# An eleventh 1 MB slot in the memory of a P buffer and a q buffer, with a free order of V groups and shorter norm, FFN and output steps

## The chip, the cores and the metric

The kernel runs on one core of a Trainium2 chip. The metric is the device time of one execution in microseconds (us), as a median of several executions. Profiled executions report a *span*, from the first to the last instruction, which is about 2 us less than the device time.

Five engines matter in the text: PE (matrix products), DVE (vector), ACT (activation), POOL, and SP, which here does nothing but issue loads. The loads themselves run on 16 DMA engines.

## The reference

Two layers of grouped-query attention over a KV cache, each followed by a SwiGLU FFN. There are four batch rows with one query token each. Both layers read **the same** K and V caches and the same weights.

```python
x = A_x                                              # (4, 1, 512) bf16
x = x + A(layernorm(x), A_k_cache, A_v_cache, A_wq, A_wo)
x = x + B(layernorm(x), B_w_gate, B_w_up, B_w_down)
x = x + A(layernorm(x), A_k_cache, A_v_cache, A_wq, A_wo)
x = x + B(layernorm(x), B_w_gate, B_w_up, B_w_down)
# A: q = x @ wq, 32 heads of 128; softmax(q k^T / sqrt(128)) v; @ wo
#    k_cache, v_cache: (4 batch, 8 kv heads, 8192, 128), each 64 MB; 4 q heads per kv head
# B: (silu(x @ w_gate) * (x @ w_up)) @ w_down, inner size 1792
```

K and V together are 128 MB. The SBUF holds a small part of that, so almost all of it is read twice: 256 blocks of 1 MB, less those blocks of V that a plan keeps in SBUF from layer 1 to layer 2.

## The kernel before

K and V come in 1 MB blocks into a pool of 10 slots. A block is half of the 8192 positions of one (batch, kv head). DVE transposes K blocks in place, PE multiplies them with a padded q (`qpad`) into four PSUM banks. When 16 K blocks of a batch are done, a softmax makes P in one of three `pp` buffers. Then V blocks are multiplied with P. A slot is free when PE has used it.

```python
KEPT = [5, 5, 4, 3]        # V blocks per batch that stay in their slots for layer 2: 17
NSLOT = 10
pool = sb("pool", [P, NSLOT, 2 * UE], BF16)          # 8 KB per partition and slot
pp = sb("pp", [P, 3, NCH * 512], BF16)               # three P buffers, 4 KB each
qpad = sb("qpad", [P, 2, NES, G, 32], BF16)          # two q buffers, 2 KB each
qs1 = sb("qs1", [P, NES, G, REP, B], BF16)           # layer-1 q of all batches, 1 KB
```

The whole program is straight-line. Before it is emitted, a planner in the kernel's own Python simulates it: each step has an engine, an assumed duration and dependencies, loads are taken in the fixed `ORDER`, and each load waits for the next free slot. The planned start times give each engine its instruction order.

```python
class Plan:
    PAGE = 6.2; PAGE_N = 256         # the plan's assumption: no more than 256 PE instructions in 6.2 us
    LOAD_LEAD = 0.8; LOAD_TAIL = 1.4
    ...
            s.start = t              # issue: when a slot is free
            dma_at = max(dma_at, t + self.LOAD_LEAD) + s.us
            s.end = dma_at + self.LOAD_TAIL
...
def load_pair(u):
    ...
        T.dma("sp", pool[:, s, :], src, sem_slot[s], writes=[f"slot{s}_0", f"slot{s}_1"])
    return PL.load(2.5, fn, u)
```

The V order follows from the `KEPT` numbers by rule: whole groups (kv heads), both halves of a group one after the other. Between the layers of one batch lies a *chain*: output projection, layer norm, FFN, layer norm, new q. The norm takes the mean with one matrix product, centers, squares, and takes the variance with a second one:

```python
def layer_norm(dep, tag):
    m = col_sum(XT, mean, "x", "mean", [dep], tag + "m")     # PE + DVE reduce
    def center(): ...                                        # xnT, dT, sqT: three DVE steps
    c = PL.add("dve", 0.5, center, [m], CHAIN)
    v = col_sum(sqT, var, "sqT", "var", [c], tag + "v")      # PE + DVE reduce
    ...
```

The softmax's maximum over partitions goes DVE reduce, PE transpose, DVE reduce of one row, PE broadcast, DVE copy. The result is transposed back by four PE instructions and written out as 4 rows.

Of the kernel before, what the change touches and what calls it, by code (L numbers as in the profile page):

```python
# [114 lines left out]
class Plan:  # L115

    HOP = 0.06
    PAGE = 6.2
    PAGE_N = 256
    LOAD_LEAD = 0.8  # L120
    LOAD_TAIL = 1.4
# [19 lines left out]
    def run(self):  # L141
# [15 lines left out]
        sp_at = 0.0  # L157
# [96 lines left out]
    def emit(self):  # L254
        for s in sorted(self.steps + self.loads, key=lambda s: (s.start, s.prio[0])):
# [3 lines left out]
ORDER = ("VKdVKqKKKVKKKKKKKgKKKKVoVVKKKVKKKKVKKKVuKVVVVKVKuKKKVVVVgoodoVKVKVKKKKKKKKKKKKKKKVKKVVVVKVVVKKV"  # L259
         "KVKVKVKVKVKKKKVVKVVKKVKVKKVVKKVVVKKKKVVKKKKVVVVKKVKVKKKVKKVKVKKVKVVVKVKKVKVKKKVVKKKKKKVKKKKVKVK"  # L260
         "VKKVVVVVVVVVVVVVVVVVVVVKVVKVKKKKKKKKKKKKKKVVVVVVVVVVVVVVVVVV")
KEPT = [5, 5, 4, 3]
NSLOT = 10
VCUT = [1, 1, 0, 1]
NTAIL = [0, 7, 5, 2]


def bass_interleave_layers__gqa_block_cached__swiglu_ffn__decode_kernel(
# [33 lines left out]
    with ExitStack() as es:  # L302
# [7 lines left out]
        pp = sb("pp", [P, 3, NCH * 512], BF16)  # L310
        qpad = sb("qpad", [P, 2, NES, G, 32], BF16)
        qs1 = sb("qs1", [P, NES, G, REP, B], BF16)
# [3 lines left out]
        identf = sb("identf", [P, P], FP32)  # L316
        selL = sb("selL", [P, 32], FP32)
        selw = sb("selw", [P, 32], FP32)
        invL = sb("invL", [P, 3, 32], FP32)
        xrow = pp[0:B, 0, 0:D]  # L320
        onesm = sb("onesm", [P, P], FP32)
        x0T = sb("x0T", [P, NQ, B], FP32)
        XT = sb("XT", [P, NQ, B], FP32)
        mean = sb("mean", [P, B], FP32)
# [5 lines left out]
        dT = sb("dT", [P, NQ, B], FP32)  # L330
        sqT = sb("sqT", [P, NQ, B], FP32)
        xnT = sb("xnT", [P, NQ * B], BF16)
        negm = sb("negm", [P, 3, 4], FP32)
        lsum = sb("lsum", [P, 3, 4], FP32)
        gm = sb("gm", [P, 1], FP32)
        gl = sb("gl", [P, 1], FP32)
        alpha = sb("alpha", [P, 3, 4], FP32)
        wl = sb("wl", [P, 4], FP32)
        rowm = sb("rowm", [1, P], FP32)
        one1 = sb("one1", [1, 1], FP32)  # L340
# [5 lines left out]
        xoT = sb("xoT", [P, NQ * B], BF16)  # L346
# [6 lines left out]
        def bank_bf(k):  # L353
# [16 lines left out]
        op("pool", lambda e: e.memset(identf[:], 0.0), writes=["identf"])  # L370
        op("pool", lambda e: e.affine_select(out=identf[:], in_=identf[:], pattern=[[-1, P]],
                                             compare_op=ALU.not_equal, fill=1.0, base=0,
                                             channel_multiplier=1),
           reads=["identf"], writes=["identf"])
        op("pool", lambda e: e.memset(qpad[:], 0.0), writes=["qpad0_0", "qpad0_1", "qpad1_0", "qpad1_1"])
        op("pool", lambda e: e.memset(oT[:], 0.0), writes=[f"oT{l}_{g}" for l in range(2) for g in range(G)])
        op("dve", lambda e: e.memset(one1[:], 1.0), writes=["one1"])
        op("dve", lambda e: e.memset(eps_sb[:], EPS), writes=["eps"])
        op("dve", lambda e: e.memset(onesm[:], 1.0 / D), writes=["onesm"])
        op("dve", lambda e: e.tensor_copy(ident[:], identf[:]), reads=["identf"], writes=["ident"])  # L380
        T.dma("sp", xrow, A_x.rearrange("b s d -> (b s) d"), sem_x, writes=["xrow"])
        nc.scalar.preload_act_table_set("natural_log_exp_and_others")

        def setup_late():
            for j in range(4):
                op("dve", lambda e: e.tensor_scalar(selL[32 * j:32 * (j + 1), :],
                                                    identf[32 * j:32 * (j + 1), 32 * j:32 * (j + 1)],
                                                    float(D), None, op0=ALU.mult),
                   reads=["identf"], writes=["selL"])
# [9 lines left out]
        def over_nq(t):  # L399
            a = t[:]  # L400
            return bass.AP(tensor=a.tensor, offset=a.offset, ap=[[a.ap[0][0], P], [0, NQ], [1, B]])
# [8 lines left out]
        def col_sum(src, dst, key_in, key_out, deps, tag):  # L410
            def mm():
                bk = pbk(tag)
                op("pe", lambda e: e.matmul(ps[:, bk * BW:bk * BW + NQ * B], lhsT=onesm[:],  # L413
                                            rhs=src[:].rearrange("p n b -> p (n b)"), start=True, stop=True),
                   reads=["onesm", key_in], writes=[f"pb{bk}"])

            def rd():
                bk = pbk(tag)
                op("dve", lambda e: e.tensor_reduce(dst[:], ps[:, bk * BW:bk * BW + NQ * B].rearrange("p (n b) -> p b n", b=B),  # L419
                                                    AX.X, ALU.add), reads=[f"pb{bk}"], writes=[key_out])  # L420
            a = PL.add("pe", 0.6, mm, deps, CHAIN, take=tag, n=8)
            return PL.add("dve", 0.17, rd, [a], CHAIN, free=tag)

        def layer_norm(dep, tag):
            m = col_sum(XT, mean, "x", "mean", [dep], tag + "m")

            def center():
                op("dve", lambda e: e.tensor_tensor(xnT[:].rearrange("p (n b) -> p n b", b=B), XT[:], over_nq(mean),
                                                    ALU.subtract), reads=["x", "mean"], writes=["xnT"])
                op("dve", lambda e: e.tensor_tensor(dT[:], XT[:], over_nq(mean), ALU.subtract),  # L430
                   reads=["x", "mean"], writes=["dT"])
                op("dve", lambda e: e.tensor_tensor(sqT[:], dT[:], dT[:], ALU.mult), reads=["dT"], writes=["sqT"])
            c = PL.add("dve", 0.5, center, [m], CHAIN)
            v = col_sum(sqT, var, "sqT", "var", [c], tag + "v")

            def root():
                op("act", lambda e: e.activation(lnv[:], var[:], ACTF.Ln, bias=eps_sb[:], scale=1.0),  # L437
                   reads=["var", "eps"], writes=["lnv"])
                op("act", lambda e: e.activation(rstd[:], lnv[:], ACTF.Exp, scale=-0.5), reads=["lnv"], writes=["rstd"])
            return c, PL.add("act", 0.55, root, [v], CHAIN)  # L440
# [39 lines left out]
        def make_qpad1(b, dep, prior):  # L480
            k = kpos[(0, b)] % 2

            def fn():
                op("dve", lambda e: e.tensor_copy(q_diag(k, 0, G), qs1[:, :, :, :, b]),
                   reads=["qs1"], writes=[f"qpad{k}_0", f"qpad{k}_1"])
            st = PL.add("dve", 0.23, fn, [dep, prior], CHAIN)
            q_ready[(0, b)] = [st, st]

        def q_first(cen, root):
# [11 lines left out]
            s1 = PL.add("dve", 0.3, scl, [mm, qs], CHAIN, free="q0")  # L501
            sp = q_spread(qT1[:], Hq * B, "qT1", [s1], "q0s")

            def cp():
                bk = pbk("q0s")
                op("dve", lambda e: e.tensor_copy(qs1[:].rearrange("p s g j b -> p (s g j b)"), bank(bk)),
                   reads=[f"pb{bk}"], writes=["qs1"])
            return PL.add("dve", 0.7, cp, [sp], CHAIN, free="q0s")

        def q_half(b, hf, mm_tag, deps, prior):  # L510
            nh = Hq // 2
            k = kpos[(1, b)] % 2
# [24 lines left out]
        def load_pair(u):  # L537
# [8 lines left out]
            return PL.load(2.5, fn, u)  # L546
# [3 lines left out]
        p_free = {0: None, 1: None, 2: None}  # L550
# [3 lines left out]
        def k_pair(u, ld, prio, prev):  # L554
            _, l, b, g, cp = u
            qbuf = kpos[(l, b)] % 2
# [29 lines left out]
        def softmax(l, b, lastq, prio):  # L586
# [17 lines left out]
            def g1():  # L604
                op("dve", lambda e: e.tensor_reduce(gm[:], negm[:, q, :], AX.X, ALU.min),
                   reads=[f"negm{q}_{a}" for a in range(4)], writes=["gm"])
            s = PL.add("dve", 0.16, g1, [mx], CHAIN)

            def g2():
                row = ps[0:1, pbk(n + "a") * BW:pbk(n + "a") * BW + P]  # L610
                op("pe", lambda e: e.matmul(row, lhsT=gm[:], rhs=identf[:], is_transpose=True, start=True, stop=True),
                   reads=["gm", "identf"], writes=[f"pb{pbk(n + 'a')}"])
            s = PL.add("pe", 0.37, g2, [s], CHAIN, take=n + "a", n=2)

            def g3():
                row = ps[0:1, pbk(n + "a") * BW:pbk(n + "a") * BW + P]
                rep = bass.AP(tensor=row.tensor, offset=row.offset, ap=[[row.ap[0][0], 1], [0, 4], [1, 32], [32, 4]])
                op("dve", lambda e: e.tensor_reduce(rowm[:].rearrange("p (i h) -> p i h", i=4), rep, AX.X, ALU.min),
                   reads=[f"pb{pbk(n + 'a')}"], writes=["rowm"])
            s = PL.add("dve", 0.7, g3, [s], CHAIN, free=n + "a")  # L620

            def g4():
                bk = pbk(n + "b")
                op("pe", lambda e: e.matmul(ps[:, bk * BW:bk * BW + 1], lhsT=rowm[:], rhs=one1[:], start=True, stop=True),
                   reads=["rowm", "one1"], writes=[f"pb{bk}"])
            s = PL.add("pe", 0.58, g4, [s], CHAIN, take=n + "b", n=8)

            def g5():
                bk = pbk(n + "b")
                op("dve", lambda e: e.tensor_copy(gm[:], ps[:, bk * BW:bk * BW + 1]), reads=[f"pb{bk}"], writes=["gm"])  # L630
            s = PL.add("dve", 0.16, g5, [s], CHAIN, free=n + "b")
# [51 lines left out]
        opj_free = [None]  # L683

# [13 lines left out]
        def v_group(l, b, g, lds, prios):  # L698
# [3 lines left out]
            for i, cp in enumerate(VCP):  # L702
# [17 lines left out]
                if not (l == 0 and (g, cp) in kept_of[b]):  # L720
# [9 lines left out]
            if l == 0 or b == B - 1:  # L730
                wdep = [w_load[f"wo{g * REP // (Hq // 4)}"]] if l == 0 else []
                return prev, oproj(l, g, [n, opj_free[0]] + wdep, prios[1])
            return prev, n

        def ffn_mm(w_sb, wname, deps, tag):
            def fn():
                bk = pbk(tag)
                for fo in range(FO):
                    for kt in range(KT):
                        op("pe", lambda e: e.matmul(ps[:, bk * BW + fo * B:bk * BW + (fo + 1) * B],  # L740
# [4 lines left out]
                           sig=(kt == KT - 1 and fo == FO - 1))  # L745
# [268 lines left out]
```

## Time and profile before

| | before |
|---|---|
| time, median | 664.6 us |
| span | 662.4 us |
| loads of K and V | 128 + 111 |
| last landing of a load | 650.2 us |
| from there to the end ("tail") | 12.2 us |

The first view is the profile's page. The digits and GB/s cover the span in 40 equal slices; the queue lines give packets, MB and the share of 16 engines' span.

```profile
span 662.4 us, 22618 instructions
PE 459.8 (69%) x10672; PEld 276.0 (42%) x10672; DVE 375.7 (57%) x568; ACT 48.6 (7%) x114; POOL 2.7 (0%) x8
DMA  8999999999999999999999999999999999999991
GB/s 341 419 420 408 408 419 405 420 419 390 391 405 419 421 419 418 405 402 414 409 421 419 419 402 414 419 419 381 403 422 420 419 419 418 379 423 419 419 419 51
q1 hardware_dynamic: 42032, 264.53, 97.6%
q8 instruction: 83, 1.36, 0.8%
```

The DMA engines are busy everywhere but in the last slice. Most slices run at 418 to 423 GB/s; 15 between the first and the last fall below, the lowest to 379. No other engine is above 69%, so the loads bound the kernel.

The windows view of two places where the rate falls. The columns are busy time of PE, PE's weight loads, DVE, ACT and POOL in the window, then the granted PE clock, the DMA share and GB/s:

```profile
454.00:456.00 2.00, 0.60 (x24) 0.34 (x32) 2.00 (x4) 0.00 (x0) 0.00 (x0) 0.50 0.99 348
...
458.00:460.00 2.00, 1.48 (x50) 1.31 (x46) 2.00 (x4) 1.62 (x5) 0.00 (x0) 0.50 0.82 221
568.00:570.00 2.00, 1.17 (x46) 1.14 (x50) 1.07 (x3) 0.00 (x0) 0.00 (x0) 0.50 0.88 369
570.00:572.00 2.00, 2.00 (x50) 0.60 (x50) 0.85 (x1) 0.00 (x0) 0.00 (x0) 0.50 0.80 266
```

Here new q, softmax and K work meet, and the DMA share falls below 1. That reads like a queue that ran empty because slots came free late.

Pieces of the timeline (start, duration, engine, line, operation; in brackets the idle time before it and what ended it). First the softmax's maximum in the last batch, then parts of the tail:

```profile
611.56 0.16 DVE L605 TENSOR_REDUCE gm<-negm 128x1 f32<-128x4 f32 x1
612.85 0.37 PE L611 MATMUL ps<-identf,gm 128*1 128x128 f32 x1
613.26 0.68 DVE L618 TENSOR_REDUCE rowm<-ps 1x128 f32<-1x512 f32 x1
614.61 0.16 DVE L630 COPY gm<-ps 128x1 f32<-128x1 f32 x1 [0.68 <-PE ps L624]
...
650.27 1.01 PE L712 MATMUL ps<-pp,pool 128*128 128x4 bf16 x32 [1.45 <-DMA pool<-in_A_v_cache_dram]
652.17 0.17 DVE L795 TENSOR_TENSOR XT<-XT,ps 128x16 f32<-128x16 f32 x1 [0.68 <-PE ps L690]
654.23 1.63 PE L740 MATMUL ps<-xnT,wg_sb 128*128 128x4 bf16 x56
657.91 1.65 PE L782 MATMUL ps<-hT,wd_sb 128*128 128x4 bf16 x56 [0.56 <-DVE hT L775]
659.83 0.59 PE L968 MATMUL ps<-ident,xoT 128*4 128x128 bf16 x4 [0.26 <-DVE xoT L795]
660.45 0.41 DVE L975 COPY pp<-ps 4x512 bf16<-4x512 bf16 x1 [0.68 <-PE ps L968]
```

The maximum takes 3.2 us from L605 to the end of L630. The last V product waits for its load. After that load nothing is fetched any more, and 12.2 us of the last FFN follow in plain sequence.

### The profile page before, as it was taken

The page shows a single profiled execution, that of the slowest core. Times are in us where ns is not written, and L with a number is a line of the kernel's source. Part 1 is how long each engine was busy: PE and PEld are TensorE (multiplying, and loading weights), DVE is VectorE, ACT ScalarE, POOL GpSimd, SP SyncE. Part 2 cuts the span into 40 slices and gives each one's busy share as a digit, 9 for nine tenths or more (in the row PEclk, how much of TensorE's full clock was granted, in tenths as well). Part 3 has the DMA queues.
Part 4 walks back from the last instruction along what each step waited for, and adds up shares of the span by engine and source line. Part 5 has one row for each costly group of instructions (what it writes and reads, how often), then busy time and mean ns, then how long its engine had stood idle before and what let it go on. Part 6 is the DMA issues. An engine that isn't in the chain of part 4 may idle for free.

```text
span 662.4 us, 22618 instructions
## 1 busy us (share of the span) xinstructions
PE 459.8 (69%) x10672; PEld 276.0 (42%) x10672; DVE 375.7 (57%) x568; ACT 48.6 (7%) x114; POOL 2.7 (0%) x8
## 2 busy tenths in 40 slices
PE   0276487477777777996676688887876857866756
PEld 0221253326522363553332354554322756523645
DVE  4377685354389815567656385467866203697202
ACT  1000300003000110001100030001101100001100
POOL 1000000000000000000000000000000000000000
PEclk9996666555566655565656555555755555576555
DMA  8999999999999999999999999999999999999991
GB/s 341 419 420 408 408 419 405 420 419 390 391 405 419 421 419 418 405 402 414 409 421 419 419 402 414 419 419 381 403 422 420 419 419 418 379 423 419 419 419 51
DMA packets 42125, 265.97 MB, mean 401 GB/s; under 512 B 4008, under 2 KB 9904, under 8 KB 10928
## 3 DMA queue, kind: packets, MB, share of 16 engines
q1 hardware_dynamic: 42032, 264.53, 97.6%
q8 instruction: 83, 1.36, 0.8%
q14 instruction: 10, 0.08, 0.0%
HBM read 264.51 MB, written 0.00 MB: 399 GB/s over the span
## 4 chain that ended last, share of the span: by engine, by line
DMA 63%; PE 22%; DVE 11%; issue 2%; ACT 1%; SPq 1%
DMA pool<-in_A_k_cache_dram 36%; DMA pool<-in_A_v_cache_dram 25%; PE ps L574 8%; DVE pool L562 8%; PE ps L712 7%; DMA wg_sb<-in_B_w_gate_dram 2%; PE ps L650 2%; PE ps L740 1%; PE ps L451 1%; DVE negm L592 1%; SPq L92 1%; ACT pp L656 1%; PE ps L690 1%; DVE pp L641 1%; PE ps L782 1%
## 5 line engine op out<-in xcount | busy, mean ns | idle before, releaser
L562 DVE STREAM_TRANSPOSE pool<-pool 128x1024 uint32<-128x1024 uint32 x256 | 304.6, 1224 | 132.8 <-DMA pool<-in_A_k_cache_dram 128.0
L574 PE MATMUL ps<-pool,qpad 32*32 32x512 bf16 x4096 | 241.1, 563 | 65.7 <-DVE pool L562 60.6
L712 PE MATMUL ps<-pp,pool 128*128 128x4 bf16 x4096 | 126.6, 166 | 64.0 <-DMA pool<-in_A_v_cache_dram 46.8
L712 PEld LDWEIGHTS ps<-pp,pool 128*128 128x128 bf16 x4096 | 118.4, 104 | 98.6 <-DMA pool<-in_A_v_cache_dram 63.1
L574 PEld LDWEIGHTS ps<-pool,qpad 32*32 32x32 bf16 x4096 | 67.9, 112 | 187.3 <-DVE pool L562 112.5
L726 DVE TENSOR_TENSOR oT<-ps,invL 128x4 bf16<-128x4 f32 x64 | 10.1, 158 | 94.7 <-PE ps L712 94.7
L596 ACT ACTIVATE pp<-ps,negm 128x512 bf16<-128x512 f32 x32 | 21.5, 685 | 359.6 <-DVE negm L592 359.6
L451 PE MATMUL ps<-xnT,wq_sb 128*128 128x4 bf16 x640 | 18.3, 166 | 23.5 <-DMA wq_sb<-in_A_wq_dram 20.1
L690 PE MATMUL ps<-oT,wo_sb 128*128 128x4 bf16 x640 | 23.4, 167 | 10.7 <-DVE oT L726 6.2
L451 PEld LDWEIGHTS ps<-xnT,wq_sb 128*128 128x128 bf16 x640 | 18.1, 104 | 26.8 <-DMA wq_sb<-in_A_wq_dram 20.2
L690 PEld LDWEIGHTS ps<-oT,wo_sb 128*128 128x128 bf16 x640 | 20.4, 105 | 19.2 <-DVE oT L726 9.7
L592 DVE TENSOR_REDUCE negm<-ps 128x1 f32<-128x512 f32 x32 | 19.8, 677 | 9.9 <-PE ps L574 9.9
L650 PE MATMUL ps<-ident,pp 128*128 128x128 bf16 x128 | 16.5, 310 | 6.1 <-ACT pp L656 3.7
L656 ACT ACTIVATE pp<-ps 128x1024 bf16<-128x1024 bf16 x16 | 16.4, 1023 | 29.6 <-PE ps L650 29.6
L437 ACT ACTIVATE lnv<-var,eps_sb 128x4 f32<-128x4 f32 x10 | 3.0, 297 | 186.6 <-DVE var L419 186.6
L650 PEld LDWEIGHTS ps<-ident,pp 128*128 128x128 bf16 x128 | 12.3, 141 | 9.5 <-ACT pp L656 4.4
L782 PE MATMUL ps<-hT,wd_sb 128*128 128x4 bf16 x280 | 8.4, 166 | 5.2 <-issue 2.4
L782 PEld LDWEIGHTS ps<-hT,wd_sb 128*128 128x128 bf16 x280 | 7.9, 104 | 6.8 <-issue 3.9
L641 DVE TENSOR_SCALAR pp<-pp,alpha 128x512 bf16<-128x512 bf16 x32 | 9.0, 342 | 1.8 <-ACT alpha L634 1.8
L740 PEld LDWEIGHTS ps<-xnT,wg_sb 128*128 128x128 bf16 x280 | 8.2, 105 | 2.2 <-issue 2.2
L740 PE MATMUL ps<-xnT,wg_sb 128*128 128x4 bf16 x280 | 8.2, 166 | 1.3 <-DMA wg_sb<-in_B_w_gate_dram 1.3
L413 PE MATMUL ps<-XT,onesm 128*128 128x16 f32 x20 | 6.0, 382 | 3.4 <-DVE XT L795 2.9
(65 smaller groups left out, 117.8 us busy)
## 6 DMA issues: line engine op xcount, KB each, us to landing
pool<-in_A_k_cache_dram SPq DMA_DIRECT2D x128, 1024.0 KB, 10.0
pool<-in_A_v_cache_dram SPq DMA_DIRECT2D x111, 1024.0 KB, 12.9
wo_sb<-in_A_wo_dram SPq DMA_DIRECT2D x4, 1024.0 KB, 17.5
wq_sb<-in_A_wq_dram SPq DMA_DIRECT2D x1, 4096.0 KB, 20.7
wg_sb<-in_B_w_gate_dram SPq DMA_DIRECT2D x2, 896.0 KB, 18.2
wu_sb<-in_B_w_up_dram SPq DMA_DIRECT2D x2, 896.0 KB, 14.9
wd_sb<-in_B_w_down_dram SPq DMA_DIRECT2D x2, 896.0 KB, 18.8
pp<-in_A_x_dram SPq DMA_DIRECT2D x1, 4.0 KB
```

Source lines behind the costliest of these rows:

```text
L451: op("pe", lambda e: e.matmul(ps[:, bk * BW + h * B:bk * BW + (h + 1) * B], lhsT=wq_sb[:, kt, h * Dh:(h + 1) * Dh], rhs=xnT[:, kt * B:(kt ...
L562: op("dve", lambda e: e.transpose(v, v), reads=[key], writes=[key])
L574: op("pe", lambda e: e.matmul(ps[32 * c:32 * (c + 1), a * BW:(a + 1) * BW], lhsT=qpad[rows, qbuf, es_, g, :], rhs=ap[h][rows, :, es_ // 2, ...
L592: op("dve", lambda e: e.tensor_reduce(negm[:, q, a:a + 1], bank(a), AX.X, ALU.max, negate=True), reads=[f"pb{a}"], writes=[f"negm{q}_{a}"])
L596: op("act", lambda e: e.activation(pblk(q)[:, :, a, :], bank(a).rearrange("p (t j) -> p t j", j=32), ACTF.Exp, bias=negm[:, q, a:a + 1], s ...
L641: op("dve", lambda e: e.tensor_scalar(seg, seg, alpha[:, q, a:a + 1], None, op0=ALU.mult), reads=[f"pp{q}_{a}", f"alpha{q}"], writes=[f"pp ...
L650: op("pe", lambda e: e.matmul(stg[:, t * P:(t + 1) * P], lhsT=pp[:, q, blk * P:(blk + 1) * P], rhs=ident[:], is_transpose=True, start=True ...
L656: op("act", lambda e: e.activation(pp[:, q, f * 1024:(f + 1) * 1024], bank_bf(bk)[:, :], ACTF.Copy), reads=[f"pb{bk}"], writes=pk(q))
L690: op("pe", lambda e: e.matmul(ps[:, OPJ * BW + nq * B:OPJ * BW + (nq + 1) * B], lhsT=wo_sb[:, h, nq * P:(nq + 1) * P], rhs=oT[:, l, h, :], ...
L712: op("pe", lambda e: e.matmul(ps[:, bk * BW:bk * BW + REP], lhsT=ap[:, t * Dh:(t + 1) * Dh], rhs=pp[:, q, col:col + REP], start=(i == 0 an ...
L740: op("pe", lambda e: e.matmul(ps[:, bk * BW + fo * B:bk * BW + (fo + 1) * B], lhsT=w_sb[:, kt, fo * P:(fo + 1) * P], rhs=xnT[:, kt * B:(kt ...
L782: op("pe", lambda e: e.matmul(ps[:, bk * BW + nq * B:bk * BW + (nq + 1) * B], lhsT=wd_sb[:, fo, nq * P:(nq + 1) * P], rhs=hT[:, fo * B:(fo ...
```

## The change

The intent: read 4 MB less, and shorten what lies between.

- Memory: the third P buffer (4 KB), the second q buffer (2 KB), `qs1` and some small tiles make room for an eleventh slot (8 KB per partition).
- 21 V blocks are kept instead of 17, so V is 107 loads instead of 111. `ORDER` is now a list of named blocks in any order. `a` is a load for layer 1, `b` for layer 2, and `c` the second use of a kept block, without a load.
- Layer norm squares x first and gets both sums from one matrix product. The maximum over partitions uses eight small DVE reductions. The FFN multiplies gate by root earlier and works in two halves at its end. The output is one transpose and 16 rows of 128.
- The planner gets new constants, and a new order made with them.

```diff
-    PAGE = 6.2
-    LOAD_LEAD = 0.8
-    LOAD_TAIL = 1.4
+    PAGE = 6.0
+    LOAD_LEAD = 1.8
+    LOAD_TAIL = 1.7
-ORDER = ("VKdVKqKKKVKKKKKKKgKKKKVoVVKKKVKKKKVKKKVuKVVVVKVKuKKKVVVVgoodoVKVKVKKKKKKKKKKKKKKKVKKVVVVKVVVKKV"
 ... (cut)
-KEPT = [5, 5, 4, 3]
-NSLOT = 10
+ORDER = ("K K wo0 K wq c161 K K x c151 K a001 K K c150 K K c350 wg0 K c020 a000 K K K K K a030 K c201 a070 "
+ ... (cut)
+         "b360 b340 b331 b320 b341 b311 b310 b361 b370 b321 b371 ")
+NSLOT = 11
+NP = 2
+NQB = 1
-        pp = sb("pp", [P, 3, NCH * 512], BF16)
-        qpad = sb("qpad", [P, 2, NES, G, 32], BF16)
-        qs1 = sb("qs1", [P, NES, G, REP, B], BF16)
+        pp = sb("pp", [P, NP, NCH * 512], BF16)
+        qpad = sb("qpad", [P, NQB, NES, G, 32], BF16)
+        def layer_norm(dep, tag):
+            def sq():
+                op("dve", lambda e: e.tensor_tensor(xx[:, 1, :, :], XT, XT, ALU.mult), reads=["x"], writes=["x2"])
+            q_ = PL.add("dve", 0.13, sq, [dep], CHAIN)
+            def mm(): ...                 # one product for the sums of x and of its square
-            s = PL.add("pe", 0.37, g2, [s], CHAIN, take=n + "a", n=2)
 ... (cut: g3, g4, g5)
+                for c in range(4):
+                    op("dve", lambda e: e.tensor_reduce(m4[:, c:c + 1], negm[32 * c:32 * (c + 1), q, :], AX.X, ALU.min),
+                for c in range(4):
+                    op("dve", lambda e: e.tensor_reduce(gm[32 * c:32 * (c + 1), :], m4[:], AX.X, ALU.min),
+            s = PL.add("dve", 1.41, g1, [mx], CHAIN)
-            pb_of[(l, b)] = b % 3
+            pb_of[(l, b)] = b % NP
```

## The prediction

> **What bounds it now.** The kernel is a stream of 1 MB loads. The page's DMA row stands at 9 in 39 of 40 slices. Two-microsecond windows show 419 to 421 GB/s wherever the queue is full, so 1 MB costs 1.0486/0.420 = 2.50 us. The Trainium skill ("DMA: Bandwidth & Descriptors", Where 436 GB/s comes from) states a ceiling of 435 GB/s; this trace holds 420, so only fewer bytes and fewer gaps can help. 264.5 MB at 420 is 630 us of the 662.4 us span. The rest, by windows: about 3 us before the queue is full; some 12 us of reduced rate inside, of which about 3 us are weights in small pieces and instruction fetch has a share, and about 7 us look like starvation (178-190, 454-460, 474, 568-576 us: 221 to 370 GB/s at under full DMA share, where K of layer 2 waits for its new q, or scores for a softmax); and a tail of about 13.5 us, in which nothing is loaded. PE (69%) and DVE (57%) matter only where a slot comes free too late.
>
> **What the change does.** By the load order, K is 128, V 107 instead of 111. 21 V blocks instead of 17 stay in SBUF for both layers. That takes 4 MB off the bound: 4 x 2.50 = -10.0 us, all on the critical path. This is the main term, and the 11th slot is what pays for it; about 5 slots are left for streaming, as before.
>
> Tail, from the timeline of the last 10 us: layer norm loses its second matrix product from the way of the gate (0.61 us, about 0.45 on the path), one 0.22 us vector step leaves the FFN and half of another, four output transposes become one (0.59 to about 0.25), the copy of 4x512 (0.41) becomes 16x128 (about 0.17). Sum about -1.5 us. Start: K is issued first and x later, about -0.4 us; q then comes about 3 us later than now (33.5 us), but 11 slots and the first weights hold about 44 us of loads, so that costs nothing.
>
> Softmax: the two PE hops (3.2 us from gm to gm, 611.6-614.8) become eight small DVE reductions, about 1.4 us. Like the shorter norms and FFN between layers (about 2 us per chain), this binds nothing directly, but frees slots sooner. Two P buffers and one q buffer add order: layer 2 of a batch must finish V before the softmax of batch+2. The new plan knows this and assumes longer transfers, so it should free slots earlier. I give it about -3 of the 7 us of starvation, with wide error.
>
> **Sum.** 664.7 - 10.0 - 1.5 - 0.4 - 3 = about 649.8 us. Range 644.5 to 656.5. Faster by over 2% (under 651.4): 0.60; within 2%: 0.38; slower: 0.02.
>
> **What would show it.** V issues 107 and read bytes 260.3 MB; full windows still 420 GB/s; the last V load landing about 13 us earlier than at 650; the tail 1.5 us shorter; the two-matmul gm exchange gone, DVE busy up by only a few us (K transposes, 304.6 us, unchanged); fewer windows under 370 GB/s at each layer-2 q.
>
> **What would make it wrong.** Longer holding of kept blocks with no more streaming slots may starve the queue in new places: then 653 to 657. A softmax held up by the two P buffers could stop all K work. If the plan meets the chip well and starvation vanishes, about 645.

## More of the kernel before

Chips differ from call to call, so each experiment is compared with runs of the kernel before on its own chip.

## The result, and the profile after

| | before | after | difference |
|---|---|---|---|
| time, median | 664.57 us (4 runs) | 654.39 us (4 runs, 653.43 to 655.18) | -10.2 us |
| span | 662.4 us | 652.3 us | -10.1 us |
| loads of K and V | 239 | 235 | -4 |
| MB on the load queue | 264.53 | 260.33 | -4.20 |
| last landing | 650.2 us | 641.0 us | -9.2 us |
| tail | 12.2 us | 11.3 us | -0.9 us |

The ratio is 0.9846, with a 95% interval of 0.9829 to 0.9863. A ratio is the mean time of one kernel's fast runs over that of the other's of the same rounds, so not quite the ratio of the medians quoted. The change is clearly faster, by 1.5%, which is inside the 2% band.

The page of the changed kernel, lines as before:

```profile
span 652.3 us, 22665 instructions
PE 434.7 (67%) x10673; PEld 268.2 (41%) x10673; DVE 376.0 (58%) x610; ACT 48.3 (7%) x114; POOL 1.8 (0%) x8
DMA  9999999999989999999999999999999999999991
GB/s 346 423 417 417 418 420 419 421 406 370 415 329 420 421 418 420 418 390 397 420 420 420 420 418 419 419 399 418 420 412 418 418 420 419 388 399 422 418 420 55
q1 hardware_dynamic: 41480, 260.33, 97.3%
q8 instruction: 83, 1.36, 0.8%
```

Full slices still run at 420, and the mean over the span is 401 GB/s in both kernels. The shallow dips of before are fewer, but there is a new deep one: slice 12 at 329. The instruction packets are 83, as before. The windows view of the dip, of the place that answers to 568 us in before, and of the last loads:

```profile
180.00:182.00 2.00, 1.32 (x45) 0.64 (x50) 0.68 (x3) 0.00 (x0) 0.00 (x0) 0.50 0.58 238
182.00:184.00 2.00, 2.00 (x47) 0.80 (x32) 1.09 (x1) 0.00 (x0) 0.00 (x0) 0.50 0.36 143
184.00:186.00 2.00, 2.00 (x70) 1.66 (x75) 1.92 (x3) 0.00 (x0) 0.00 (x0) 0.50 0.52 156
...
568.00:570.00 2.00, 0.48 (x18) 0.48 (x18) 2.00 (x4) 0.00 (x0) 0.00 (x0) 0.50 0.68 274
570.00:572.00 2.00, 2.00 (x60) 1.02 (x64) 2.00 (x5) 0.00 (x0) 0.00 (x0) 0.50 0.63 229
...
636.00:638.00 2.00, 1.31 (x50) 1.22 (x46) 0.00 (x0) 0.00 (x0) 0.00 (x0) 0.50 0.71 295
638.00:640.00 2.00, 1.36 (x39) 1.19 (x39) 0.17 (x1) 0.00 (x0) 0.00 (x0) 0.50 0.34 131
```

As a mean over the 16 DMA engines, the stream lost 3.44 us at 180 to 186 us: 420 less the rate, over 420, times 2 us, summed over the three windows. This is where layer 2 of the first batch waits for its q. The last two rows matter later: the queue does not end at once, but over some 4 us, with a part of the DMA engines still at work.

The timeline of the tail:

```profile
641.25 0.99 PE L691 MATMUL ps<-pp,pool 128*128 128x4 bf16 x32
643.13 0.17 DVE L789 TENSOR_TENSOR xx<-xx,ps 128x16 f32<-128x16 f32 x1 [0.69 <-PE ps L669]
644.70 1.66 PE L720 MATMUL ps<-xnT,wg_sb 128*128 128x4 bf16 x56 [0.49 <-DVE xnT L427]
648.18 1.65 PE L773 MATMUL ps<-hT,wd_sb 128*128 128x4 bf16 x56 [0.33 <-DVE hT L765]
650.12 0.28 PE L928 MATMUL ps<-ident,xoT 128*16 128x128 bf16 x1 [0.28 <-DVE xoT L789]
650.43 0.21 DVE L935 COPY pp<-ps 16x128 bf16<-16x128 bf16 x1 [0.37 <-PE ps L928]
```

From the new x to the gate it is 1.57 us (before: 2.06), from the gate to the down product 3.48 (before: 3.68), and the output steps are shorter by 0.5. The groups view confirms the softmax's small steps, eight per softmax at about 145 ns:

```profile
L607 DVE TENSOR_REDUCE gm<-m 32x1 f32<-32x4 f32 x32 | 4.7, 147 | 1.1
L604 DVE TENSOR_REDUCE m<-negm 32x1 f32<-32x4 f32 x32 | 4.6, 143 | 0.9
```

One more reading can be taken from the trace: the times at which the loads land, one after the other. The trace holds 16 records for each load, one for each part of it; the load has landed with the last of them. Where the queue is full, a 1 MB block lands 2.485 us after the one before it. With the usual step of each kind of weight, all loads after the first should take 627.4 us in before and 617.4 us in after. Measured from the first landing to the last, they take 644.2 and 635.4 us. So the landings slip by 16.9 us in before and by 17.9 us in after. In both, most slips come while, by the issue times, the queue is several loads deep. The change took away 9.9 us of nominal stream, and the slips stayed. They are more than twice the starvation that I had read from the windows. What these slips are is the question for the experiments.

### The profile page after: what moved, and what is told of

It is laid out like the page before. It is cut to its first block, busy times and chain, and to the rows that moved or that the text cites. A ratio compares the mean times of both kernels' runs of the same rounds, so it can differ in the third digit from the quotient of the medians.

```text
span 652.3 us, 22665 instructions
## 1 busy us (share of the span) xinstructions
PE 434.7 (67%) x10673; PEld 268.2 (41%) x10673; DVE 376.0 (58%) x610; ACT 48.3 (7%) x114; POOL 1.8 (0%) x8
## 3 DMA queue, kind: packets, MB, share of 16 engines
q1 hardware_dynamic: 41480, 260.33, 97.3%
q8 instruction: 83, 1.36, 0.8%
## 4 chain that ended last, share of the span: by engine, by line
DMA 53%; PE 25%; DVE 12%; issue 6%; SPq 2%; ACT 2%
DMA pool<-in_A_k_cache_dram 35%; DMA pool<-in_A_v_cache_dram 18%; PE ps L572 11%; DVE pool L560 9%; PE ps L691 8%; SPq L92 2%; PE ps L628 2%; ACT pp L634 2%; PE ps L452 1%; DVE negm L590 1%; PE ps L720 1%; PE ps L773 1%; PE ps L669 1%; DVE pp L619 1%; PE ps L418 0%
## 5 line engine op out<-in xcount | busy, mean ns | idle before, releaser
L572 PE MATMUL ps<-pool,qpad 32*32 32x512 bf16 x4096 | 226.2, 531 | 83.7 <-DVE pool L560 64.2
L691 PE MATMUL ps<-pp,pool 128*128 128x4 bf16 x4096 | 124.4, 166 | 66.9 <-DMA pool<-in_A_v_cache_dram 33.4
L572 PEld LDWEIGHTS ps<-pool,qpad 32*32 32x32 bf16 x4096 | 69.5, 108 | 208.3 <-DVE pool L560 123.1
L705 DVE TENSOR_TENSOR oT<-ps,invL 128x4 bf16<-128x4 f32 x64 | 10.2, 160 | 114.2 <-PE ps L691 114.1
L452 PEld LDWEIGHTS ps<-xnT,wq_sb 128*128 128x128 bf16 x640 | 17.9, 104 | 9.3 <-issue 5.9
L628 PEld LDWEIGHTS ps<-ident,pp 128*128 128x128 bf16 x128 | 12.2, 139 | 6.0 <-DVE selw L644 2.5
L720 PE MATMUL ps<-xnT,wu_sb 128*128 128x4 bf16 x280 | 8.8, 166 | 1.6 <-issue 0.7
```

The source lines that it names most:

```text
L452: op("pe", lambda e: e.matmul(ps[:, bk * BW + h * B:bk * BW + (h + 1) * B], lhsT=wq_sb[:, kt, h * Dh:(h + 1) * Dh], rhs=xnT[:, kt * B:(kt ...
L572: op("pe", lambda e: e.matmul(ps[32 * c:32 * (c + 1), a * BW:(a + 1) * BW], lhsT=qpad[rows, qbuf, es_, g, :], rhs=ap[h][rows, :, es_ // 2, ...
L628: op("pe", lambda e: e.matmul(stg[:, t * P:(t + 1) * P], lhsT=pp[:, q, blk * P:(blk + 1) * P], rhs=ident[:], is_transpose=True, start=True ...
L691: op("pe", lambda e: e.matmul(ps[:, bk * BW:bk * BW + REP], lhsT=ap[:, t * Dh:(t + 1) * Dh], rhs=pp[:, q, col:col + REP], start=(i == 0 an ...
L720: op("pe", lambda e: e.matmul(ps[:, bk * BW + (fo - f0) * B:bk * BW + (fo - f0 + 1) * B], lhsT=w_sb[:, kt, fo * P:(fo + 1) * P], rhs=xnT[: ...
```

## The experiments

Twelve kernels were run. My theory after the result: **A**, the gain is the bytes, and the slips come from instruction fetch and a little from late slots, both left as they were. The rivals are named in each run's expectation.

| label | time, median | before in the same rounds | ratio, 95% interval | last landing |
|---|---|---|---|---|
| kept17 | 661.93 | 664.38 | 0.9961 (0.9945 to 0.9976) | 649.0 |
| tail_only | 663.90 | 664.38 | 0.9992 (0.9977 to 1.0006) | 650.8 |
| loads_only | 628.54 | 664.38 | 0.9458 (0.9440 to 0.9475) | 624.7 |
| loads_pe | 642.61 | 664.38 | 0.9670 (0.9655 to 0.9685) | 638.9 |
| old_memory_21 | 685.52 | 663.88 | 1.0324 (1.0279 to 1.0370) | 676.4 |
| old_memory_17 | 667.45 | 663.88 | 1.0045 (1.0022 to 1.0068) | 654.5 |
| slots10 | 699.39 | 663.88 | 1.0527 (1.0502 to 1.0553) | 687.3 |
| loads_half_pe | 635.50 | 663.88 | 0.9569 (0.9554 to 0.9584) | 631.7 |
| tail_grouped | 654.10 | 664.67 | 0.9844 (0.9829 to 0.9858) | 640.6 |
| small_only | 669.74 | 664.67 | 1.0084 (1.0068 to 1.0101) | 658.5 |
| fetch_plan_21 | 658.93 | 664.67 | 0.9914 (0.9894 to 0.9934) | 648.9 |
| fetch_plan_22 | 662.12 | 664.67 | 0.9965 (0.9948 to 0.9982) | 648.1 |

The last landing is from one profiled run of each; the others have spreads of up to 7 us in time (old_memory_21), so differences of landings are read to about a microsecond. Differences in time between experiments of different calls are good to about half a microsecond, as the kernel before was at 664.4, 663.9 and 664.7 us in the three.

### The loads by themselves: loads_only, loads_pe, loads_half_pe

All three copy x to the output. Their outputs are wrong, which doesn't matter for the times.

```diff
         PL.run()
-        PL.emit()
+        for s in sorted(PL.loads, key=lambda s: s.start):
+            s.fn()                       # the loads alone; a slot waits for its previous load
+        # loads_pe: PE_N = 10672; loads_half_pe: PE_N = 5336; loads_only: not there
+        for i in range(PE_N):
+            op("pe", lambda e: e.matmul(ps[:, 0:REP], lhsT=ident[:], rhs=ident[:, 0:REP], start=True, stop=True),
+               reads=["ident"], writes=["pb0"], sig=(i == PE_N - 1))
```

> Wrong on purpose: only the changed kernel's 247 loads in its order, each slot waiting for nothing but its previous load; no compute, output is a copy of x. Theory A (the slips inside the stream come from what the compute does: instruction fetches that sit on one DMA engine for 1.07 us each, and slots freed late): no slips, last landing at about 623 us (5.65 us for the first and 617.4 us for the rest at the nominal time of each), time about 627. Rival B (the slips of some 18 us are the memory's or the DMA's own): last landing stays near 638 to 641.

> Wrong on purpose: the loads alone as in loads_only, and 10672 matmuls on PE on a constant tile that wait for no load, so that PE's instructions are fetched while the loads run. Theory A1 (instruction fetch alone makes most of the slips, because a load lands only when the slowest of 16 DMA engines is done): about as many 16 KB fetches as in the changed kernel (some 83), and the last landing 4 to 18 us later than in loads_only. Rival A2 (fetch costs only its bytes, 1.36 MB at 420 GB/s, 3.2 us; slots freed late make the rest): last landing at most 3.5 us later than loads_only.

> Wrong on purpose: loads_pe with half of the matmuls (5336, so about 41 fetches of 16 KB). Theory A (each fetch holds up the landing front by a fixed amount; 83 of them cost 14.1 us over loads_only, 628.5 us): about half, 635 to 636.5, and the last landing near 632. Rival B (a cost of being interleaved at all, not of the number): 640 or more; rival C (they are hidden in slack until they are many): under 632.

Without compute the slips are nearly gone: the last landing is at 624.7 us, with 1.6 us of slips, where the changed kernel has 641.0. The memory delivers 420 GB/s from end to end. With PE running through 10672 matmuls that depend on no load, the time rises by 14.07 us. With half of them it rises by 6.96 us. The pages differ in the line of instruction packets; first loads_pe's, then loads_half_pe's:

```profile
q8 instruction: 83, 1.36, 0.9%
```

```profile
q8 instruction: 41, 0.67, 0.4%
```

14.07 us over 83 fetches and 6.96 us over 41 are both 0.170 us each. (loads_half_pe ran on another chip than the other two. By the ratios to before on each chip its cost is 7.4 us, 0.18 each, so the second figure is known to about 0.5 us.) So the cost is in proportion to the number of fetches. It is also in proportion to PE's matmuls, which were halved with them; what tells these two apart follows below. It is not the bytes of the fetches: 16 KB at 420 GB/s are 0.039 us, 3.2 us for all 83. Nor is it slots: no load waits for compute in these kernels. The Trainium skill ("Runtime: NRT & Kernel Launch", Instruction fetch mechanics) says that each engine's instruction memory is refilled in blocks of 16 KiB, 256 instructions. This trace agrees: PE has 21,346 instructions with its weight loads, which is 83.4 times 256, and there are 83 packets of 16 KB. The page calls the cost "mostly hidden". Whether it is hidden for PE's own work, no run here tests; for a kernel that is bound by its loads, it is about 14 us of 654.

Why four times its bytes? The same skill ("DMA: Bandwidth & Descriptors", Why a DMA increments its semaphore by 16 and not by 1) says that a load runs on up to 16 DMA engines that finish independently, and has landed when the last has. This trace agrees: it has 16 landing records for each load. A fetch is one packet, and in the changed kernel such a packet mostly took 1.02 to 1.11 us, where an ordinary 8 KB packet of a load takes 0.31. If it sits on one engine, it delays that engine by a microsecond or more, and every load lands that much later, though 15 engines were in time. The end of the stream shows engines that are behind. The windows of loads_only (columns: DVE, ACT, POOL, clock, DMA share, GB/s; before them it was at full rate):

```profile
622.00:624.00 2.00, 0.00 (x0) 0.00 (x0) 0.00 (x0) 1.00 0.43 176
624.00:626.00 2.00, 0.00 (x0) 0.00 (x0) 0.00 (x0) 1.00 0.00 1
```

The windows of loads_pe, with the two PE columns in front:

```profile
630.00:632.00 2.00, 0.00 (x0) 0.00 (x0) 0.00 (x0) 0.00 (x0) 0.00 (x0) 1.00 0.81 336
632.00:634.00 2.00, 0.00 (x0) 0.00 (x0) 0.00 (x0) 0.00 (x0) 0.00 (x0) 1.00 0.50 209
634.00:636.00 2.00, 0.00 (x0) 0.00 (x0) 0.00 (x0) 0.00 (x0) 0.00 (x0) 1.00 0.51 213
636.00:638.00 2.00, 0.00 (x0) 0.00 (x0) 0.00 (x0) 0.00 (x0) 0.00 (x0) 1.00 0.28 119
```

In loads_only all engines stop within about 2 us. In loads_pe the share stands at 0.50 for 4 us: the packets in flight there number eight, so eight engines have done their part and eight are still working. That fits fetches that take turns on eight engines: eight times 0.170 is 1.36 us, and in kept17, below, the landings slip by 1.26 to 1.52 us at a time, eleven times, at distances of 49 to 73 us, which is about eight fetches.

The packets in the trace don't say on which engine they ran, but the 16 landing records of each load in loads_pe settle it. Count those that come over 0.9 us after the load's first. In loads_only there is never more than one. In loads_pe there are none before any fetch. After the 1st, 3rd, 4th and 5th fetch there are 1, 3, 4 and 5, and so on up to 8 in the load at 54.8 us, after the eighth. The ninth fetch makes no ninth late record: it sets one of the eight back a second time, to 3.15 us. From 522 us to the end, after the last fetch at 512.2 us, all 48 loads look alike: eight records within 0.6 us of the first, and eight 5.3 to 7.5 us after it. So the fetches fall on eight engines in turn, and the rival, that PE's own work slows the loads, doesn't explain delays that come one record at a time.

By the mean of the eight latest records, counted from the first landing, loads_pe ends 13.7 us behind loads_only; times 8, over 83, that is 1.33 us of one engine's time for each fetch. This answers the question of the four times, as an estimate: 16 KB at a sixteenth of 420 GB/s would be 0.62 us, so a fetch takes twice its share of an engine, and with eight engines instead of 16 that doubles again.

So theory A1 held for fetch, and A2 (only its bytes) fell. For the real kernels this gives a floor, which is an estimate from runs on different chips: the changed kernel's loads and its fetches alone land last at 638.9 us. The changed kernel is at 641.0, so only 2.1 us of it are late slots. For before the floor is four loads later, 638.9 + 4 x 2.485 = 648.8, and it is at 650.2: 1.4 us of late slots.

### What the four blocks are worth: kept17

```diff
-"K K wo0 K wq c161 K K x c151 ... K c020 a000 ... K c201 a070 ... K c350 ..."
+# c020, c161, c201, c350 become b020, b161, b201, b350: loaded for layer 2 again,
+# each at the place in the order of layer 2 that the planner found best; 17 kept
```

> The changed kernel with four of its 21 kept V blocks loaded twice again (17 kept, as before the change), 11 slots. Theory A (the gain is bytes: 4 MB at 2.50 us each, and the landing slips inside the stream are the same with or without them): about 664, 10 us above the changed kernel and level with the kernel before; last landing about 651. Rival B (the eleventh slot and the plan gained by fewer starved stretches, bytes are not all): with 17 kept and 11 slots there is slack to spare and the time stays well below the kernel before, at 655 to 659.

It took 661.9 us: between the two. Against the changed kernel that is 7.5 us for 4 MB, not 10. The landings say why. Its last landing, 649.0, is 0.2 us from the floor of 648.8: with slack to spare, late slots cost kept17 next to nothing. At the dip of the changed kernel it stands at:

```profile
182.00:184.00 2.00, 2.00 (x53) 0.92 (x38) 1.10 (x1) 0.00 (x0) 0.00 (x0) 0.50 0.72 299
184.00:186.00 2.00, 2.00 (x65) 1.71 (x69) 1.91 (x3) 0.00 (x0) 0.00 (x0) 0.50 0.85 262
```

So keeping four more blocks gained 9.9 us of stream and gave back some 2 us as late slots. The dip at 180 us is deeper for it: 143 GB/s in the middle window against 299. The landings there show the price: the two after 185.3 us come 3.67 and 3.48 us after the ones before them in the changed kernel, 2.2 us more than two steps of 2.485, and 2.47 and 2.49 us after in kept17, with nothing lost. (At the second of the two only one of the 16 records is set back, as a fetch does it, so not all of the 2.2 us need be late slots.) Theory A's "the same slips with or without" was a little wrong, and rival B (655 to 659, bytes are not nearly all) was wrong by more.

### What pays for the bytes: old_memory_21, old_memory_17, slots10

```diff
 # old_memory_21: the changed kernel; old_memory_17: kept17
-NSLOT = 11
-NP = 2
-NQB = 1
+NSLOT = 10
+NP = 3
+NQB = 2
 # slots10: the changed kernel with NSLOT = 10 alone
```

> The changed kernel, 21 blocks kept and its load order, but the memory split as before the change: 10 slots, three P buffers, two q buffers. Theory A (21 kept blocks need the eleventh slot): the stream starves and the time is well above the changed kernel, by 10 us or more (664 or more, so all of the 10 us are lost again). Rival B (the slot is not what pays for the bytes, the new order is): within 3 us of the changed kernel, 654 to 657.

> The kernel kept17 (17 kept, 661.9 us with 11 slots, two P buffers and one q buffer) with the old split: 10 slots, three P buffers, two q buffers. Theory A (kept17 had no starvation left to remove, its last landing was where loads and instruction fetch alone would put it; with one slot less a little comes back): 662 to 667. Rival B (P and q buffers had been holding the stream back, a third and a second one help): under 661.

> The changed kernel with 10 slots, two P buffers and one q buffer: old_memory_21 without the extra P and q buffers. If P and q buffers matter little, the same as old_memory_21 within 3 us; if the third P and second q buffer carry part of what the slot carried, slower than old_memory_21 by 5 us or more.

With 21 blocks kept and the old split of the memory, the time is 685.5 us, 31 us above the changed kernel: theory A, and more of it than expected. With ten slots and the smaller P and q buffers it is 699.4, over 5 us slower still, as the second case of its expectation has it. So at 21 kept blocks and with this load order a slot is worth 45 us (slots10 to the changed kernel), the third P and the second q buffer together 14 us (slots10 to old_memory_21), and the exchange of one for the other 31. The windows of old_memory_21 show what that is; the place is the same as above:

```profile
182.00:184.00 2.00, 2.00 (x37) 0.64 (x38) 0.04 (x1) 0.00 (x0) 0.00 (x0) 0.50 0.20 74
184.00:186.00 2.00, 2.00 (x63) 1.65 (x60) 2.00 (x2) 0.00 (x0) 0.00 (x0) 0.50 0.40 86
```

At 17 kept blocks the same exchange is worth 5.5 us (old_memory_17, 667.5, to kept17, 661.9), at the upper edge of its theory A. One reservation: in these runs the planner makes the order of each engine anew for the changed memory, but the order of loads was searched for eleven slots. A search for ten would find something better: before itself, with ten slots and its own order, runs 664. So 31 us is what this load order needs the slot for, not what the best plans of both differ by.

### The small steps: tail_only, small_only

tail_only keeps the old steps for the first norm, the softmax and the four chains, and takes the new ones for the last FFN and the output. small_only takes all new steps. Both have before's order, slots and buffers.

```diff
 # tail_only (in the kernel before)
-        s = ffn(s, f"f{b}")
-        cen, root = layer_norm(s, f"q{b}n")
+        s = ffn_old(s, f"f{b}")                     # the old functions under new names
+        cen, root = layer_norm_old(s, f"q{b}n")
         s = ffn(s, "z", dst=xoT, dkey="xo")         # the new function, in the tail alone
 # small_only: the new layer_norm, ffn, maximum and output everywhere
```

> The kernel before with the new layer norm, FFN and output transpose for the last FFN alone (the four earlier ones and the softmax keep the old steps). Theory A (the tail's steps are worth what their durations say, 1.0 to 1.5 us): 663.1 to 663.7 against 664.6, and the time from the start of the last V matmuls to the end falls from 12.2 us to about 11. Rival B (hidden, nothing gained): within 0.3 us of the kernel before.

> The kernel before with the new steps of layer norm, FFN, softmax maximum and output alone; its order, 10 slots, three P and two q buffers stay. Theory A (these steps are worth the tail, about 1 us, and nothing else): 663 to 664. Rival B (shorter chains also free slots sooner and take away starvation): 661 or less. Rival C (the old order was fitted to the old lengths, and the stream now starves in a new place): 666 or more.

tail_only: the profile shows a tail of 11.1 us instead of 12.2, as theory A has it. The time fell by 0.5 us in the medians, and its interval reaches from -0.23% to +0.06%, so the time alone does not settle it. small_only was a surprise: 669.7 us, 5 us **slower** than before, though its chains are shorter. Its last landing is 8 us later than before's. By the time, rival C held (666 or more): the load order was fitted to the old lengths. With other lengths the planner puts the steps of each engine in another order, and the same loads now starve in new places (windows of its profiled run, which was the slowest of its four):

```profile
230.00:232.00 2.00, 2.00 (x45) 0.68 (x30) 0.81 (x1) 0.94 (x1) 0.00 (x0) 0.50 0.55 229
232.00:234.00 2.00, 2.00 (x73) 1.72 (x78) 0.17 (x1) 0.00 (x0) 0.00 (x0) 0.50 0.62 135
```

So part of what the new order in the change does is probably to fit the new steps again; no run tries the new order with the old steps.

### Can the rest be had: tail_grouped, fetch_plan_21, fetch_plan_22

In the changed kernel three output projections fall close together at the end. tail_grouped takes the last 12 loads in whole groups:

```diff
-"b330 b360 b340 b331 b320 b341 b311 b310 b361 b370 b321 b371"
+"b330 b331 b360 b361 b340 b341 b310 b311 b320 b321 b370 b371"
```

> The changed kernel with its last 12 V loads put in whole groups (both halves of a group one after the other), same loads otherwise. Theory A (in the changed kernel three output projections fall together at the end and hold back the last V block, which started 0.2 us after its load's landing but behind 1.2 us of instruction wait inside a projection): about 653.4, 1 us less than the changed kernel's 654.4. Rival B (the last V block waits for the load, not for PE): within 0.4 us of it.

654.1 us, as the changed kernel within the noise: rival B. In the changed kernel the last V product started at 641.25, 0.23 us after its load landed at 641.02, so there was nothing for PE to give back.

fetch_plan_21 and fetch_plan_22 let the planner count each fetch as 0.165 us of the load stream, and take an order of loads from a new search under it.

```diff
+    FETCH = 0.165
-    LOAD_TAIL = 1.7
+    LOAD_TAIL = 1.3
                 page_at = max(there, page_at + self.PAGE)
+                dma_at += self.FETCH
-            return PL.load(2.515, fn, u)
+            return PL.load(2.49, fn, u)
 # ORDER: searched anew (21 and 22 blocks kept)
```

> The changed kernel with a plan that counts instruction fetch: each 16 KB fetch of PE moves the landing front by 0.165 us (13.6 us in 83), 2.49 us a load, and the load order searched anew under it; 21 blocks kept, same code else. Theory A (the loads and fetch alone end at 638.9 us; the changed kernel ends its loads 2.1 us later through late slots, which a plan that knows of the fetch can take back): last landing near 639, time about 652 to 653. Rival B (the remaining slips are not of this kind): 654 or more.

> As fetch_plan_21 with 22 blocks kept, so one load less (2.5 us). Theory A (a plan that counts the fetch leaves room for one more kept block): 650 to 652, about 2 us below fetch_plan_21. Rival B (the eleven slots are full at 21): no better than fetch_plan_21, starvation eats the 2.5 us.

Both missed: 658.9 and 662.1 us, 4.5 and 7.7 us slower than the changed kernel, though still faster than before. fetch_plan_21 starves at 180 to 186 us again (windows of its profiled run, the slowest of its six):

```profile
180.00:182.00 2.00, 1.12 (x35) 0.48 (x35) 0.94 (x4) 0.00 (x0) 0.00 (x0) 0.50 0.58 229
182.00:184.00 2.00, 0.93 (x24) 0.45 (x29) 1.20 (x2) 0.00 (x0) 0.00 (x0) 0.50 0.36 152
184.00:186.00 2.00, 2.00 (x63) 1.16 (x48) 1.18 (x2) 0.00 (x0) 0.00 (x0) 0.50 0.06 20
```

It lost 4.1 us there, more than the changed kernel. A single number for the fetch is not a model of a front where eight engines in 16 fall behind one at a time, the planner's assumed landing (`LOAD_TAIL` 1.3 instead of 1.7) was more hopeful than the changed kernel's, and the new search may simply have ended in a worse order. Which of these did the harm was not tried, so it stays open. No version that beats the changed kernel was found.

## Why the prediction was right or wrong

The measured 654.4 us lies in the stated range (644.5 to 656.5), 4.6 us above the forecast of 649.8. The range was wide enough for one wrong term: the two mechanisms that were right (bytes and slot) carried the result. The class was "within 2%", to which 0.38 had been given, against 0.60 for faster.

- **The stream of loads bounds the kernel: right.** With no compute at all the loads still take until 624.7 us, and with the fetches until 638.9, of the changed kernel's 641.0.
- **-10.0 us for 4 MB: right as a cost, shown by the count.** The queue moved 260.33 MB, the nominal stream is 9.9 us shorter, and full windows still run at 420. kept17 adds that 4 MB back for 7.5 us, because the kept blocks themselves cost about 2 us of late slots.
- **The eleventh slot pays for it: right.** Without it the order with 21 kept blocks takes 685.5 us. The fear that two P buffers could stop all K work did not come true at eleven slots; with ten slots the third P and second q buffer are worth 14 us.
- **-0.4 us at the start: right.** The first landing came at 5.65 instead of 5.99 us. The late x made q 4.2 us later (first score product at 37.75 instead of 33.52) and cost nothing, as the loads were issued ahead.
- **-1.5 us in the tail: too much, -0.9.** From the last V product to the end the profile shows 12.17 to 11.05 us, -1.1: 0.49 from x to the gate, 0.20 from gate to down product, and the output. The rest is that this last product began 0.23 us after its landing instead of 0.05.
- **-3 of 7 us of starvation: wrong, and the term that moved the result off the middle.** There were no 7 us to take. Late slots were 1.4 us in before. The dips that I read as starvation are mostly those DMA engines running dry that were ahead of the ones with the fetches, and the landing is not set by those. At before's dip from 183 to 193 us, four loads in a row, the first of each load's 16 records lost 3.2 us against steps of 2.485, but the last, which is the landing, lost less than 0.1; at 454 to 464 us it was 2.8 and 0.2, and at 569 to 579 us 3.0 and 0.7. The windows show the mean of all engines and cannot tell these apart; the landings can, and a kernel with the loads alone. Late slots are 2.1 us after the change, so this term was +0.7 and not -3. The text had named this case under what would make it wrong: kept blocks that starve the queue in new places, 653 to 657.

The sum of what was measured: 9.9 for the bytes, 0.3 for the start and 0.9 for the tail, less 1.0 by which the slips grew (16.9 to 17.9 us), is 10.1 us, the difference of the spans. Of the 1.0 the floors give 0.7 to late slots; they leave out that the first landings differ. The small differences are from one profiled run each, so a few tenths of each are noise.

The prediction also had instruction fetch "has a share" of the reduced rate. It had the thing and not its size: it named it beside about 3 us, and it is 14.

## What to carry to other kernels

When a kernel is bound by its loads, run the loads alone, and then the loads with the instructions but without the dependencies: the two differences say what the memory, the instruction stream and the schedule each cost, which the profile of the real kernel cannot. A straight-line program of many small PE instructions pays for each 256 of them on the load stream, here 0.170 us, so fewer and larger PE instructions may be worth more than PE's busy share suggests; no run here tried it. A dip in the rate is a mean over 16 engines; whether it costs anything is read from the last landing record of each load. A searched order belongs to the step lengths and buffers it was searched for: shorter steps under the old order made this kernel 5 us slower.

## What the Trainium skill lacked or had wrong

- "Runtime: NRT & Kernel Launch", Instruction fetch mechanics, calls the cost of crossing a 16 KiB boundary one tail-bump, "mostly hidden". For the loads of a kernel that fills the DMA queue it is not hidden: 83 fetches cost 14.07 us, 41 cost 6.96 us, 0.170 us each, where their bytes at 420 GB/s would take 0.039.
- "DMA: Bandwidth & Descriptors", Queues, rings and completion order, names refill among what runs on row 14 of the same 16 engines, but gives it no cost. Here one fetch packet of 16 KB mostly took 1.02 to 1.11 us, against 0.31 for an 8 KB packet of a load, and cost its engine 1.33 us. The profile lists the 83 packets under q8 and 10 others under q14; how its numbers relate to the page's rows, no run here shows.
- On which engines fetches go, no page says. In loads_pe they fell on eight of the 16 in turn, and these eight were the last ones at work for 4 us at the end.
- "DMA: Bandwidth & Descriptors", Where 436 GB/s comes from, says that for transfers from HBM the HBM side binds, at about 358 GB/s. Read alone this misleads for one core: the page's own note under its measured table gives 358 for two cores that stream at once, and 425 for one core and 16 MB. Here, with one core in use, the page of loads_only shows 419 to 426 GB/s in all slices but those of the weights and the two ends.
